# Funnel attention followed by a multiplicative FFN: one interleaved pipeline in place of three stages, with PV turned round and the transposes of its output done by DMA

## Chip, cores, metric

The kernel runs on one core of a Trainium2 chip. The metric is the device time of one execution in microseconds, measured on the chip; the profiles come from the hardware profiler, and in them time counts from the first instruction. Executions are called fast or slow: for a program on one core, slow means more than 1.5% above the fastest run of the same kernel.

Abbreviations: PE is TensorE (PEld its weight loads), DVE is VectorE, ACT is ScalarE, POOL is GpSimd, SP is SyncE; SPq is SP's issuing of DMAs. T is the product w3·w_out. A *pair* is two heads of one batch element; there are 32 pairs.

## The reference, cut to what matters

```python
# q, k, v: (8, 8, 1152, 64) float32, scaled by 0.1
q_pool = q.reshape(B, H, S // 2, 2, D).mean(axis=3)        # 576 queries
scores = q_pool @ k.T / sqrt(64)
attn   = softmax(scores)                                   # over 1,152 keys
x      = (attn @ v), heads side by side                    # (4608, 512)
a = x @ w1 ; b = x @ w2                                    # (4608, 1024)
out = ((a * b) @ w3) @ w_out                               # float32 (4608, 512)
```

Both kernels use that (a·b)·w3·w_out = (a·b)·T with T = w3·w_out, calculated once. Both calculate in fp16 with fp32 sums, and neither subtracts the maximum.

## The kernel before

There are three stages, one after the other. First T: w3 is transposed block by block on PE and multiplied by w_out. Then attention, by head pairs; this is the loop of one pair, shortened:

```python
# (cut: pools, tiles)
for h0 in range(0, H, 2):
    for b in range(B):
        # k, q, v of two heads: rows of 64 elements
        nc.gpsimd.dma_start(out=kpair[:, :, u, :], in_=k[b, h].rearrange("(c p) d -> p c d", p=128))
        # ... the same for q and v ...
        for jt in range(NJ):                       # nine transposes by DMA
            nc.sync.dma_start(out=kT2[:, jt, :], in_=kpair[:, jt, :, :], transpose=True)
        # pooling of q on PE (18 small matmuls), then one DVE copy to qpT2
        for g0 in range(0, FLAT, 512):             # 11 groups of 512 columns, two heads each
            # scores: k stationary (64 rows x 128), pooled q moving
            nc.scalar.activation(out=eT[...], in_=psc[...], func=AF.Exp, ...)
            for jt in range(done_av, jdone):       # PV at once: v stationary, exponentials moving
                nc.tensor.matmul(poT[u][:, i0:i0 + ln], vt_[u][:, jt, 0:D + 1], eT[...], ...)
        # result and sum of exponentials to DRAM
        nc.sync.dma_start(out=xT32d[h, :, b * Sq:(b + 1) * Sq], in_=otmp[0:64, :])
        nc.sync.dma_start(out=zAll[h, b * Sq:(b + 1) * Sq], in_=otmp[64:65, :])
    # every eight pairs: zAll back from DRAM, reciprocal, to DRAM, back as a broadcast;
    # xT32d back; product into xT (fp16, features on partitions)
```

Here PV gives 64 features on partitions and 576 queries along the free axis. The sum of exponentials of a query then lies in row 64, and must reach all 64 rows; this kernel sends it there through DRAM. The last stage is the FFN over nine units of 512 tokens, each 96 matmuls of 512 columns.

The softmax here doesn't subtract the row's maximum and nothing guards it: scores larger than these inputs give would overflow.

Of the kernel before, what the change touches and what calls it, by code (L numbers as in the profile page):

```python
# [7 lines left out]
DBG = set()  # L9

FP32 = mybir.dt.float32
FP16 = mybir.dt.float16
BF16 = mybir.dt.bfloat16
F32R = mybir.dt.float32r
AF = mybir.ActivationFunctionType
ALU = mybir.AluOpType


def _make_pool_matrix(nc, ptile):
    nc.gpsimd.memset(ptile, 0.5)  # L20
    nc.gpsimd.affine_select(
        out=ptile, in_=ptile, compare_op=ALU.is_ge, fill=0.0,
        base=0, channel_multiplier=1, pattern=[[-2, ptile.shape[1]]],
    )
    nc.gpsimd.affine_select(
        out=ptile, in_=ptile, compare_op=ALU.is_gt, fill=0.0,
        base=2, channel_multiplier=-1, pattern=[[2, ptile.shape[1]]],
    )


def _make_identity(nc, ident):
    nc.gpsimd.memset(ident, 0.0)
    nc.gpsimd.affine_select(
        out=ident, in_=ident, compare_op=ALU.not_equal, fill=1.0,
        base=0, channel_multiplier=1, pattern=[[-1, ident.shape[1]]],
    )


def _pieces(lo, hi, *bounds):
    cuts = set()  # L40
    for bnd in bounds:
        x = (lo // bnd + 1) * bnd
        while x < hi:
            cuts.add(x)
            x += bnd
    edges = [lo] + sorted(cuts) + [hi]
    return [(edges[i], edges[i + 1] - edges[i]) for i in range(len(edges) - 1)]


def _interleave(items, keyfn):  # L50
    ev = [x for x in items if keyfn(x) % 2 == 0]
    od = [x for x in items if keyfn(x) % 2 == 1]
    out = []
    for i in range(max(len(ev), len(od))):
        if i < len(ev):
            out.append(ev[i])
        if i < len(od):
            out.append(od[i])
    return out
# [3 lines left out]
def kernel(  # L63
# [12 lines left out]

    B, H, S, D = q.shape
    Sq = S // 2
    NJ = S // 128
    dm = H * D  # L80
    dff = moe_w1.shape[1]
    NT = B * Sq
    NC = dm // 128
    NF = dff // 128

    SCALE = float(D) ** -0.5
    SCL = 16.0
    AG = 1024
    NPSC = 2
    FLAT = NJ * Sq  # L90

    const = ctx.enter_context(tc.tile_pool(name="const", bufs=1))
    big = ctx.enter_context(tc.tile_pool(name="big", bufs=1))

    ident16 = const.tile([128, 128], FP16)
    _make_identity(nc, ident16)
    pool16 = const.tile([128, 64], FP16)
    _make_pool_matrix(nc, pool16)

    xT = big.tile([128, NC, NT], FP16)  # L100
    w1sb = big.tile([128, NC, dff], FP16)
    nc.gpsimd.dma_start(out=w1sb, in_=moe_w1.rearrange("(c p) f -> p c f", p=128))
    w2sb = big.tile([128, NC, dff], FP16)
    nc.gpsimd.dma_start(out=w2sb, in_=moe_w2.rearrange("(c p) f -> p c f", p=128))
    T16 = big.tile([128, NF, dm], FP16)

    zpool = ctx.enter_context(tc.tile_pool(name="zpool", bufs=1, space=bass.MemoryType.DRAM))
    zAll = zpool.tile([H, NT], FP32)
    xT32d = zpool.tile([H, 64, NT], FP32)


    with tc.tile_pool(name="t_sb", bufs=1) as tsb, \
         tc.tile_pool(name="t_ps", bufs=2, space=bass.MemoryType.PSUM) as tps:
        w3sb = tsb.tile([128, NF, dff], FP16)
        nc.gpsimd.dma_start(out=w3sb, in_=moe_w3.rearrange("(c p) f -> p c f", p=128))
        wosb = tsb.tile([128, NF, dm], FP16)
        nc.gpsimd.dma_start(out=wosb, in_=moe_w_out.rearrange("(c p) f -> p c f", p=128))
        w3T = tsb.tile([128, NF, dff], FP16)
        for a in range(NF):
            pt = tps.tile([128, 1024], FP32, tag="w3tp")  # L120
            for c in range(NF):
                nc.tensor.transpose(pt[:, c * 128: c * 128 + 128].bitcast(FP16)[:, 0:128],  # L122
                                    w3sb[:, c, a * 128: a * 128 + 128], ident16)
            nc.vector.tensor_copy(out=w3T[:, a, :], in_=pt.bitcast(FP16).rearrange("p (c j) -> p c j", j=256)[:, :, 0:128])
        for ft in range(NF):
            pT = tps.tile([128, dm], FP32, tag="pT")
            for a in range(NF):
                nc.tensor.matmul(pT, w3T[:, a, ft * 128: ft * 128 + 128], wosb[:, a, :],  # L128
                                 start=(a == 0), stop=(a == NF - 1))
            nc.scalar.copy(out=T16[:, ft, :], in_=pT)  # L130

    with tc.tile_pool(name="att_sb", bufs=2) as sb, \
         tc.tile_pool(name="att_sb3", bufs=3) as sb3, \
         tc.tile_pool(name="att_dram", bufs=4, space=bass.MemoryType.DRAM) as sdram, \
         tc.tile_pool(name="att_norm", bufs=1) as npool, \
         tc.tile_pool(name="att_ps", bufs=1, space=bass.MemoryType.PSUM) as ps:
        for h0 in range(0, H, 2):
            for b in range(B):
                hpair = [h0, h0 + 1]
                qt_, vt_ = [], []  # L140
                kpair = sb3.tile([128, NJ, 2, D], FP16, tag="kpair")
                for u, h in enumerate(hpair):
                    qtile = sb3.tile([128, NJ, D], FP16, tag=f"qtile{h % 2}")
                    vtile = sb3.tile([128, NJ, D + 1], FP16, tag=f"vtile{h % 2}")
                    nc.gpsimd.dma_start(out=kpair[:, :, u, :], in_=k[b, h].rearrange("(c p) d -> p c d", p=128))  # L145
                    nc.gpsimd.dma_start(out=qtile, in_=q[b, h].rearrange("(c p) d -> p c d", p=128))  # L146
                    nc.vector.memset(vtile[:, :, D:D + 1], 1.0)  # L147
                    nc.gpsimd.dma_start(out=vtile[:, :, 0:D], in_=v[b, h].rearrange("(c p) d -> p c d", p=128))  # L148
                    qt_.append(qtile); vt_.append(vtile)

                kT2 = sb3.tile([128, NJ, 128], FP16, tag="kT2")
                for jt in range(NJ):
                    nc.sync.dma_start(out=kT2[:, jt, :], in_=kpair[:, jt, :, :], transpose=True)  # L153

                pqpt = ps.tile([128, 1024], FP32, tag="psc", bufs=NPSC)
                pqp = pqpt[:, 0:Sq]
                for jt in range(NJ):
                    nc.tensor.matmul(pqp[0:64, jt * 64: jt * 64 + 64],  # L158
                                     qt_[0][:, jt, :], pool16, start=True, stop=True)
                    nc.tensor.matmul(pqp[64:128, jt * 64: jt * 64 + 64],  # L160
                                     qt_[1][:, jt, :], pool16, start=True, stop=True)
                qpT2 = sb3.tile([128, Sq], FP16, tag="qpT2")
                nc.vector.tensor_copy(out=qpT2, in_=pqp)

                eT = sb.tile([128, 2, FLAT], FP16, tag="eT")
                poT = [ps.tile([65, 1024], FP32, tag="poT", bufs=2, name=f"poT{_u}") for _u in range(2)]
                done_av = 0
                for g0 in range(0, FLAT, 512):
                    glen = min(512, FLAT - g0)
                    psc = ps.tile([128, 2, 512], FP32, tag="psc", bufs=NPSC)  # L170
                    for (st, ln) in _pieces(g0, g0 + glen, Sq):
                        jt = st // Sq
                        i0 = st - jt * Sq
                        for u in range(2):
                            nc.tensor.matmul(  # L175
                                psc[:, u, st - g0: st - g0 + ln],
                                kT2[u * 64: u * 64 + 64, jt, :],
                                qpT2[u * 64: u * 64 + 64, i0:i0 + ln],
                                start=True, stop=True)
                    nc.scalar.activation(out=eT[:, :, g0:g0 + glen], in_=psc[:, :, 0:glen],  # L180
                                         func=AF.Exp, bias=0.0, scale=SCALE)
                    jdone = (g0 + glen) // Sq
                    for jt in range(done_av, jdone):
                        for (i0, ln) in _pieces(0, Sq, 512):
                            for u in range(2):
                                nc.tensor.matmul(  # L186
                                    poT[u][:, i0:i0 + ln], vt_[u][:, jt, 0:D + 1],
                                    eT[:, u, jt * Sq + i0: jt * Sq + i0 + ln],
                                    start=(jt == 0), stop=(jt == NJ - 1))
                    done_av = jdone  # L190
# [26 lines left out]
    if "nomoe" in DBG:  # L217
        nc.vector.memset(out[0:128, :], 0.0) if False else None
        return
# [60 lines left out]
```

## Time and profile before

The median is 853.73 us (four runs, 849.86 to 854.45).

| Stage | us | PE busy | granted clock |
|---|---|---|---|
| weights and T | 0 to 50 | 41% | 1.0 |
| attention | 50 to 658 | about 67% | 0.73 |
| FFN | 658 to 853 | 96% | 0.98 |

The page of the kernel before, the rows of 40 equal slices (21.3 us each; a digit is a tenth):

```profile
PE   0777878866657885566788556568810899999998
...
PEclk9998876866666777766768877586865899999999
DMA  9999999999899999999989998963055011111111
```

PE is only full in the last quarter, the FFN. In attention its granted clock lies between a half and full, and the DMA row reads 8 or 9 until about 555 us. The windows of two stages of the kernel before (busy us, number of instructions, then clock, DMA share and GB/s):

```profile
50.00:650.00 600.00, 399.86 (x2868) 190.33 (x2868) 105.15 (x164) 321.18 (x352) 171.62 (x174) 0.73 1.05 104
660.00:853.00 193.00, 185.78 (x852) 83.53 (x851) 53.23 (x73) 63.61 (x108) 0.00 (x0) 0.98 0.13 50
```

The columns of busy time are PE, PEld, DVE, ACT, POOL. The DMA share is the sum of the times of packets over the time of the 16 engines, and can be above 1. The DMA queues of the kernel before (packets, MB, share of 16 engines), then its chain of waits by engine:

```profile
q0 software_dynamic: 227392, 33.57, 61.0%
q1 hardware_dynamic: 58944, 47.67, 25.2%
...
PE 47%; DMA 17%; ACT 13%; SPq 11%; DVE 6%; issue 4%; POOL 1%; DVEq 0%; ACTq 0%; POOLq 0%
```

The timeline of SP in the kernel before (start us, duration) shows nine transposes of a pair, then its stores:

```profile
113.41 11.33 SPq L153 DMA_TRANSPOSE kT_1174<-kpair  x9
124.84 0.53 SPq L196 DMA_DIRECT2D xT32d<-otmp  x1
125.42 0.43 SPq L197 DMA_DIRECT2D zAll<-otmp  x1
```

### The profile page before, as it was taken

To read this page: it belongs to the slowest core of one execution; us is meant where nothing else is said; L and a number is where in the kernel's file an instruction comes from. 1 tells how busy PE (TensorE), PEld (TensorE's weight loads), DVE (VectorE), ACT (ScalarE), POOL (GpSimd) and SP (SyncE) were. 2 spreads that over 40 slices of the span, in tenths; PEclk is the share of its full clock that TensorE was granted. 3 is DMA by queue.
4 is the path that set the end of the run, shared out by engine and by line. 5 is a ranking of instruction groups with operands and counts; after the bars stand their busy time and mean duration, and the time that the engine had idled before them with its cause. 6 is when DMAs were issued, how large, how long until landed. Compare 5 with 4: busy or idle time off the path is not lost.

```text
span 853.1 us, 10018 instructions
## 1 busy us (share of the span) xinstructions
PE 606.2 (71%) x3872; PEld 285.8 (33%) x3872; DVE 166.3 (19%) x252; ACT 391.5 (46%) x469; POOL 193.9 (23%) x205
## 2 busy tenths in 40 slices
PE   0777878866657885566788556568810899999998
PEld 0433433422323332232334222233300344444443
DVE  0211111103121111322211032220003322222222
ACT  0157656644445664444566444456600333333332
POOL 4512525342213243221324322020000000000000
PEclk9998876866666777766768877586865899999999
DMA  9999999999899999999989998963055011111111
GB/s 167 170 91 79 115 98 119 94 134 150 141 107 85 84 93 118 162 143 102 89 77 97 127 147 148 86 66 48 15 128 111 25 50 57 54 50 59 53 50 50
DMA packets 286384, 81.88 MB, mean 96 GB/s; under 512 B 273472, under 2 KB 274496, under 8 KB 285312
## 3 DMA queue, kind: packets, MB, share of 16 engines
q0 software_dynamic: 227392, 33.57, 61.0%
q1 hardware_dynamic: 58944, 47.67, 25.2%
q8 instruction: 30, 0.49, 0.2%
q14 instruction: 18, 0.15, 0.1%
HBM read 86.13 MB, written 19.17 MB: 123 GB/s over the span
## 4 chain that ended last, share of the span: by engine, by line
PE 47%; DMA 17%; ACT 13%; SPq 11%; DVE 6%; issue 4%; POOL 1%; DVEq 0%; ACTq 0%; POOLq 0%
ACT eT L180 13%; SPq L153 10%; PE psc L175 8%; PE pa L230 7%; PE po L244 7%; PE pb L234 7%; DMA zsb<-zAll 3%; DMA wosb<-in_moe_w_out_dram 3%; DVE xT L214 3%; PE pT L128 2%; DMA x_3888<-xT32d 2%; DMA x_1472<-xT32d 2%; DMA x_2680<-xT32d 2%; DMA x_5096<-xT32d 1%; DVE otmp L195 1%
## 5 line engine op out<-in xcount | busy, mean ns | idle before, releaser
L180 ACT ACTIVATE eT<-psc 128x1024 f16<-128x1024 f32 (+1 forms) x352 | 321.9, 954 | 249.0 <-PE psc L175 242.8
L186 PEld LDWEIGHTS <-vtile 128*65 128x65 f16 x1152 | 131.3, 127 | 221.7 <-issue 170.2
L145 POOL DMA_DIRECT2D kpair<-in_k_dram x64 | 63.8, 997 | 275.0 <-DMA zAll<-otmp 164.6
L230 PE MATMUL pa<-xT,w1sb 128*128 128x512 f16 x288 | 75.6, 384 | 42.1 <-DVE xT L214 40.6
L238 ACT COPY asb<-pa 128x512 f32<-128x512 f32 x72 | 42.1, 585 | 119.2 <-PE pa L230 119.2
L146 POOL DMA_DIRECT2D qtile<-in_q_dram x64 | 63.5, 1004 | 63.2 <-PE pqpt L160 57.5
L239 DVE TENSOR_TENSOR gT<-pb,asb 128x512 f16<-128x512 f32 x72 | 49.8, 691 | 130.0 <-PE pb L234 128.5
L234 PE MATMUL pb<-xT,w2sb 128*128 128x512 f16 x288 | 74.8, 381 | 0.0
L148 POOL DMA_DIRECT2D vtile<-in_v_dram x64 | 63.6, 999 | 42.2 <-DVE vtile L147 23.7
L244 PE MATMUL po<-T_75,gT 128*128 128x512 f16 x288 | 63.6, 379 | 0.0
L234 PEld LDWEIGHTS <-w2sb 128*128 128x128 f16 x288 | 28.3, 98 | 75.3 <-issue 41.8
L247 ACT ACTIVATE osb<-po 128x512 f32<-128x512 f32 x36 | 21.5, 597 | 49.0 <-PE po L244 47.0
L230 PEld LDWEIGHTS <-w1sb 128*128 128x128 f16 x288 | 28.4, 98 | 36.2 <-issue 3.0
L244 PEld LDWEIGHTS <-gT 128*128 128x128 f16 x288 | 28.1, 98 | 34.0
L122 PE MATMUL pt<-ident_61,w3sb 128*128 128x128 f16 x64 | 5.8, 259 | 25.5 <-DMA w3sb<-in_moe_w_dram 25.5
L130 ACT CAST T_75<-pT 128x512 f16<-128x512 f32 x8 | 4.7, 585 | 40.5 <-PE pT L128 40.5
L204 DVE RECIPROCAL rsb<-zsb 128x72 f32<-128x72 f32 x4 | 2.4, 603 | 75.1 <-DMA zsb<-zAll 75.1
L128 PE MATMUL pT<-wosb,w3T 128*128 128x512 f16 x64 | 14.6, 379 | 1.7 <-DMA wosb<-in_moe_w_out_dram 1.7
L158 PE MATMUL pqpt<-pool_66,qtile 128*64 128x64 f16 x288 | 15.0, 198 | 0.8 <-ACT T_75 L130 0.8
L160 PE MATMUL pqpt<-pool_66,qtile 128*64 128x64 f16 x288 | 15.1, 199 | 0.0
L122 PEld LDWEIGHTS <-w3sb 128*128 128x128 f16 x64 | 5.3, 119 | 26.3 <-DMA w3sb<-in_moe_w_dram 25.5
L175 PE MATMUL psc<-qpT_4082,kT_4053 64*128 64x512 f16 (+7 forms) x36 | 5.0, 360 | 12.3 <-DVE vtile L147 12.3
(250 smaller groups left out, 723.7 us busy)
## 6 DMA issues: line engine op xcount, KB each, us to landing
kpair<-in_k_dram POOLq DMA_DIRECT2D x64, 144.0 KB, 5.5
qtile<-in_q_dram POOLq DMA_DIRECT2D x64, 144.0 KB, 5.6
vtile<-in_v_dram POOLq DMA_DIRECT2D x64, 144.0 KB, 5.6
xT32d<-otmp SPq DMA_DIRECT2D x64, 144.0 KB
rb<-rAll SPq DMA_DIRECT2D x8, 1152.0 KB
out_dram<-osb SPq DMA_DIRECT2D x36, 256.0 KB
w3sb<-in_moe_w_dram POOLq DMA_DIRECT2D x1, 2048.0 KB, 21.7
x_1467<-xT32d SPq DMA_DIRECT2D x1, 1152.0 KB
```

What stands on the lines that cost most here:

```text
L145: nc.gpsimd.dma_start(out=kpair[:, :, u, :], in_=k[b, h].rearrange("(c p) d -> p c d", p=128))
L146: nc.gpsimd.dma_start(out=qtile, in_=q[b, h].rearrange("(c p) d -> p c d", p=128))
L148: nc.gpsimd.dma_start(out=vtile[:, :, 0:D], in_=v[b, h].rearrange("(c p) d -> p c d", p=128))
L153: nc.sync.dma_start(out=kT2[:, jt, :], in_=kpair[:, jt, :, :], transpose=True)
L175: nc.tensor.matmul(psc[:, u, st - g0: st - g0 + ln], kT2[u * 64: u * 64 + 64, jt, :], qpT2[u * 64: u * 64 + 64, i0:i0 + ln], start=True, s ...
L180: nc.scalar.activation(out=eT[:, :, g0:g0 + glen], in_=psc[:, :, 0:glen], func=AF.Exp, bias=0.0, scale=SCALE)
L186: nc.tensor.matmul(poT[u][:, i0:i0 + ln], vt_[u][:, jt, 0:D + 1], eT[:, u, jt * Sq + i0: jt * Sq + i0 + ln], start=(jt == 0), stop=(jt == ...
L230: nc.tensor.matmul(pa[:, 0:tl], w1sb[:, mc, ft * 128: ft * 128 + 128], xT[:, mc, t0: t0 + tl], start=(mc == 0), stop=(mc == NC - 1))
L234: nc.tensor.matmul(pb[:, 0:tl], w2sb[:, mc, ft * 128: ft * 128 + 128], xT[:, mc, t0: t0 + tl], start=(mc == 0), stop=(mc == NC - 1))
L238: nc.scalar.copy(out=asb[:, 0:tl], in_=pa[:, 0:tl])
L239: nc.vector.tensor_mul(out=gT[:, ft, 0:tl], in0=pb[:, 0:tl], in1=asb[:, 0:tl])
L244: nc.tensor.matmul(po[0:ttl, :], gT[:, ft, tt: tt + ttl], T16[:, ft, :], start=(ft == 0), stop=(ft == NF - 1))
```

## The change

The intent is to leave no stage in which PE waits:

- *Loads in wide rows.* A partition takes 9 (or 18) neighbouring rows of k, v (or q): 1,152 B or more in SBUF, where it was 128 B.
- *One transpose instruction* for the nine blocks of kT; pooling on DVE before a transpose of q.
- *PV turned round.* The exponentials are stationary (128 queries), v with its column of ones moves (65 columns). The result has queries on partitions, so 1/z is a per-partition number beside it. Normalisation is a reciprocal and a product on DVE; DMA transposes then write xT. Nothing goes through DRAM.
- *Lag.* A flat stream of 324 chunks of 512 columns over all pairs; PV runs one iteration (two chunks) behind the exponentials.
- *Weaving.* Batches come first, so tokens are complete early, and steps of T and of the FFN (four matmuls each) are put between attention steps, 1.2 per iteration. Seven of the nine units run inside the loop.

```diff
-                    nc.gpsimd.dma_start(out=kpair[:, :, u, :], in_=k[b, h].rearrange("(c p) d -> p c d", p=128))
+            out=kst[P].rearrange("p u j d -> p u (j d)"),
+            in_=k[b, h0:h0 + 2].rearrange("u (p j) d -> p u (j d)", j=NJ))
-                for jt in range(NJ):
-                    nc.sync.dma_start(out=kT2[:, jt, :], in_=kpair[:, jt, :, :], transpose=True)
+        nc.sync.dma_start_transpose(out=kT[P], in_=kc.rearrange("p j u d -> p (j u d)"))
...
-                                    poT[u][:, i0:i0 + ln], vt_[u][:, jt, 0:D + 1],
-                                    eT[:, u, jt * Sq + i0: jt * Sq + i0 + ln],
+        for u in range(2):
+            for i in range(5):
+                f = 128 * i if i < 4 else SQ - 128
+                nc.tensor.matmul(
+                    po[P][:, u, VW * i:VW * i + D + 1],
+                    er[:, u, r + f:r + f + 128],
+                    vts[P % 4][:, u, j, 0:D + 1], ...)
...
+        nc.vector.reciprocal(out=rz, in_=acc[:, :, :, D:D + 1])
+        nc.vector.tensor_tensor(out=xn..., in0=acc[:, :, :, 0:D], in1=rz.to_broadcast(...), op=ALU.mult)
+        nc.sync.dma_start_transpose(out=xT[:, hp, n0:n0 + 512]..., in_=xn[:, 0:4]...)
...
+    for it in range(NIT):                       # 162 iterations
+        if it == 3:
+            w3_transpose()                      # 2 DMA transposes of 32 blocks each, on SP
+        if it == 6:
+            filler.append(gen_T())
+        # (cut) a unit of the FFN joins the filler as soon as its tokens are complete
+        scores(2 * it)
+        expo(2 * it)
+        scores(2 * it + 1)
+        expo(2 * it + 1)
+        # (cut) loads and transposes two pairs ahead
+        credit = min(credit + 24 / 20.0, 2.4)
+        while (SQ * (nextJ + 1) - 1) // CH <= 2 * it - 1:
+            attend(nextJ)                       # PV of one block of keys
+            nextJ += 1
+        fill(3)                                 # steps of T and the FFN, by credit
```

## The prediction

> **What bounds the kernel now.** It has three stages in series. The timeline in 40 slices and the stage windows show: 0 to 50 us weights and the product w3·w_out; 50 to 658 us attention, 32 head pairs at about 19 us each; 658 to 853 us the FFN. Only the last is full: matmuls of 512 columns follow each other every 216 ns at a granted clock near 1.0. In attention PE is busy about 70% at a clock of 0.70 to 0.76, ACT 55%. The reasons there are data movement: DMA engines are 90% busy or more in nearly every slice, the software queue alone 61% of 16 engines (227,392 packets, nearly all under 512 B); each pair issues nine 128x128 DMA transposes of 1.23 us on SP, about 13.5 us with its stores; and four times a head pair's normalisation goes through DRAM (loads of zAll and xT32d, 7 to 13 us each in the chain of waits). The chain is PE 47%, DMA 17%, ACT 13%, SP queue 11%.
>
> **What the change does.** Loads become rows of 1,152 B in SBUF instead of 128 B, so the software queue should fall from 61% to a small share. The DRAM round trip of x, z and 1/z goes. PV is turned: 1,152 weight loads and 331,776 columns [...] become 2,880 pairs of weight load and 65-column matmul. In this trace 128x128 weight loads hide behind 128-column matmuls (56 ns pitch in the w3 transposes), and two 64-column pairs pass in about 30 ns (pooling). So I estimate 30 to 45 ns a pair, 86 to 130 us. A 128-wide weight load took 98 ns against about 110 for 65-wide ones[...]. Pooling leaves PE (288 pairs) for a DVE add. The FFN (864 matmuls, 187 us) is unchanged, but seven of nine units and T are woven into the attention loop.
>
> **Cost.** The loop has 162 iterations. ACT: two exponentials at 0.92 us pitch, 1.84 us. PE: scores 0.47, PV 0.55 to 0.8, 1.2 filler steps of 0.866: 2.05 to 2.3 us. So PE sets the pace just above ACT: 162 x 2.25 = 365 us, plus about 1 us a pair for the single po bank and DVE queueing: 32 us. Outside it: start until the first scores 17 us; a stall near pair 3, since the 64 blocks of the w3 transposes stand before its kT on SP, 25 us; the tail of two units and the rest of a third, 52 steps x 0.866 plus drains, 52 us. Sum 491 us. Nearly all of the gain lies on the critical path, because the old FFN stage stops being a stage.
>
> **Predicted: 490 us, 8 in 10 between 440 and 590.** Faster by over 2%: 0.96; within 2%: 0.02; slower: 0.02.
>
> **What would show it.** PE busy 80% or more in the loop, clock above 0.9; ACT about 80% there; DMA share about a third; one PV pair near 30 to 45 ns start to start; the tail near 50 us.
>
> **What would make it wrong.** SP. Per pair it now issues about 18 blocks' worth of transposes in four instructions. [...] If 1.23 us holds per 128x128 block, SP needs over 20 us a pair and the time is 700 us; if most of it is fixed per instruction, 8 to 10 us and it hides. No trace here tells which. Also PV pairs at 60 ns or more, or the clock falling to half in the loop (PE would then need 4 us an iteration), would add 50 to 150 us.

For the old PV the trace gives an estimate: at the 216 ns measured for 512 columns, its 331,776 columns take 140 us. That a transpose might cost by block stands as an assumption: before the change only the 1.23 us of one block was measured.

## More of the kernel before

The wait that costs PE most in attention, from the waits of PE in the kernel before (us in total, times, longest):

```profile
PE psc L175 <- DVE vtile L147: 108.8, 28, 12.3
```

At the start of nearly every pair PE waits for DVE, which copies the pooled queries behind the epilogue of the pair before. (The view names L147, the memset of a later v tile; in the timelines the copy, L163, ends 0.05 us before PE starts.) Most of these waits last 1.74 us.

Nine last 4.1 to 12.3 us, 75.7 us together, and they come three pairs in a row, at each of the first three ways through DRAM: in the timeline of DVE the copy stands, as in the program, behind an instruction of the way through DRAM that waits for its DMA (21.72 us in this one):

```profile
194.18 0.60 DVE L204 RECIPROCAL rsb<-zsb 128x72 f32<-128x72 f32 x1 [21.72 <-DMA zsb<-zAll]
...
195.97 0.74 DVE L163 CAST qpT_1666<-pqpt 128x576 f16<-128x576 f32 x1
```

PE starts the scores of that pair at 196.76 us, after 9.47 us idle. Elsewhere one pair follows the other every 14.6 to 17.4 us; those nine take 18.7 to 25.7 us.

## The result

The changed kernel takes 498.14 us (median of four, 497.42 to 498.83). The ratio to the kernel before is 0.5832 (95% interval 0.5811 to 0.5853). Ratios here are the mean time of one kernel's fast runs over that of the other's in the same rounds, so not quite the ratio of the medians quoted.

The page of the changed kernel, the same rows (slices of 12.4 us):

```profile
PE   0062009987999999999999999999999999999996
...
PEclk9996558998999999999999999999999999999998
DMA  8999999899899898999998989998999254012213
```

From the eleventh slice on PE is at 90% or more, but for the last. What is left lies at the start: in the first six slices, about 75 us, PE is busy for about 12 us. The windows of the loop and of the tail of the changed kernel (columns as above):

```profile
120.00:440.00 320.00, 311.49 (x3984) 160.44 (x3982) 148.51 (x252) 258.79 (x269) 42.87 (x63) 1.00 0.90 129
448.00:497.00 49.00, 43.76 (x202) 19.48 (x200) 13.03 (x19) 14.14 (x24) 0.00 (x0) 0.97 0.25 57
```

In the loop PE is busy 311.49 of 320 us, 97%, at full clock, and ACT 81%. The tail is 49 us. The queues and the chain of the changed kernel:

```profile
q0 software_dynamic: 25168, 33.56, 46.2%
q1 hardware_dynamic: 91840, 30.43, 39.8%
...
PE 69%; DMA 15%; ACT 7%; issue 5%; DVE 3%; POOL 1%; ACTq 0%; DVEq 0%; POOLq 0%
```

There are nine times fewer packets on the software queue, with the same bytes. Its share has only come down by a quarter, but of a shorter span: in time, 61.0% of 853 us was 520 us of packets and 46.2% of 497 us is 230 us. And what PE waited for most, from its waits in the changed kernel (us in total, times, longest):

```profile
PE psc L143 <- DMA qT<-qp: 32.3, 2, 25.7
PE pT L218 <- DMA w3T<-w3h: 28.5, 1, 28.5
```

The first line holds two waits, 25.7 us until the first scores and 6.6 us before the second pair. The second is one wait for the transposed w3.

Two timelines of the changed kernel show why. On PE, the first step of T, which the program puts behind iteration 6, waits for the transposed w3, and everything behind it in PE's order waits too:

```profile
45.55 0.73 PE L163 MATMUL po<-vt_77,er 128*128 128x65 f16 x10
74.76 1.89 PE L218 MATMUL pT<-wosb,w3T 128*128 128x512 f16 x4 [28.48 <-DMA w3T<-w3h]
```

On SP, the two long transposes of w3 stand behind qT of the third pair, and before kT and qT of the fourth (L105 and L123 below); PE waited for neither of these two.

```profile
35.45 9.50 SPq L123 DMA_TRANSPOSE qT<-qp  x1
44.99 31.93 SPq L204 DMA_TRANSPOSE w3T<-w3h  x2
77.04 1.20 SPq L180 DMA_TRANSPOSE xT<-xn  x1
78.28 1.23 SPq L183 DMA_TRANSPOSE xT<-xn  x1
79.62 1.29 SPq L105 DMA_TRANSPOSE kT<-kc  x1
80.96 1.27 SPq L123 DMA_TRANSPOSE qT<-qp  x1
```

The same lines settle the question that the prediction left open. A transpose of nine blocks (L105) holds SP for 1.29 us here; one of four blocks (L180) 1.20 us; one of half a block (L183) 1.23 us. Before, one block took 1.23 us. So, up to nine blocks, the time on SP does not go by block. It is no constant either. Over all 32 pairs the instruction of nine blocks took (the view of its line: shortest/median/longest in ns, then first and last start in us)

```profile
L105 SPq DMA_TRANSPOSE kT<-kc x32: 1295/2129/5904, 5.9 to 417.3; - x32
```

and at the start, where loads are queued as well, the one for qT took up to 10.85 us. From issue to landing qT took 2.7 us at the least, 6.8 us in the median and 23.9 us at the most. What held SP back was not isolated.

So the 497 us of the profiled span divide as follows: 26 us to the first scores, 35 us of two gaps, 387 us for the 162 iterations, 49 us of tail. Over iterations 24 to 140 the exponentials of successive iterations start 2.40 us apart on average.

Where do the 355 us come from? The FFN stage of 195 us is no longer a stage; the attention stage of 608 us has become a loop that contains most of the FFN. The profiles alone do not say what part of the change did how much. The experiments ask that.

### The profile page after: what moved, and what is told of

It reads as the page before. It is cut to its first block, busy times and chain, and to the rows that moved or that the text cites. A ratio compares the mean times of both kernels' runs of the same rounds, so it can differ in the third digit from the quotient of the medians.

```text
span 496.9 us, 11617 instructions
## 1 busy us (share of the span) xinstructions
PE 415.5 (84%) x4960; PEld 213.4 (43%) x4960; DVE 182.8 (37%) x313; ACT 327.2 (66%) x349; POOL 69.4 (14%) x105
## 3 DMA queue, kind: packets, MB, share of 16 engines
q0 software_dynamic: 25168, 33.56, 46.2%
## 4 chain that ended last, share of the span: by engine, by line
PE 69%; DMA 15%; ACT 7%; issue 5%; DVE 3%; POOL 1%; ACTq 0%; DVEq 0%; POOLq 0%
PE po L163 18%; PE psc L143 16%; PE pa L231 11%; PE pb L242 11%; PE pp L250 10%; ACT er L149 7%; DMA w3T<-w3h 6%; DMA w3h<-in_moe_w_dram 4%; DMA kst<-in_k_dram 2%; PE pT L218 2%; DVE xn L175 2%; DMA qst<-in_q_dram 2%; DVE rz L173 1%; DMA xT<-xn 0%; POOL kst L83 0%
## 5 line engine op out<-in xcount | busy, mean ns | idle before, releaser
L149 ACT ACTIVATE er<-psc 128x1024 f16<-128x1024 f32 x324 | 311.8, 1023 | 133.2 <-PE psc L143 132.8
L143 PE MATMUL psc<-qT,kT 64*128 64x512 f16 (+7 forms) x1152 | 114.5, 291 | 42.9 <-DMA qT<-qp 32.3
L163 PEld LDWEIGHTS <-er 128*128 128x128 f16 x2880 | 98.5, 98 | 48.4 <-issue 35.5
L143 PEld LDWEIGHTS <-kT 64*128 64x128 f16 x1152 | 44.3, 95 | 125.3 <-issue 91.9
L250 PE MATMUL pp<-T_73,gT 128*128 128x512 f16 x288 | 70.1, 379 | 0.0
L83 POOL DMA_DIRECT2D kst<-in_k_dram x32 | 23.2, 724 | 273.6 <-DVE kc L103 248.8
L238 DVE COPY asb<-pa 128x512 f32<-128x512 f32 x56 | 38.7, 691 | 57.8 <-PE pa L231 57.5
L218 PE MATMUL pT<-wosb,w3T 128*128 128x512 f16 x64 | 17.3, 400 | 28.5 <-DMA w3T<-w3h 28.5
L163 PE MATMUL po<-vt_77,er 128*128 128x65 f16 x720 | 31.2, 199 | 1.5 <-DVE xn L175 1.5
L163 PE MATMUL po<-vt_78,er 128*128 128x65 f16 x720 | 29.7, 194 | 0.9 <-DVE xn L175 0.9
L163 PE MATMUL po<-vt_80,er 128*128 128x65 f16 x720 | 29.4, 194 | 1.2 <-DVE xn L175 1.2
L163 PE MATMUL po<-vt_79,er 128*128 128x65 f16 x720 | 29.4, 194 | 1.2 <-DVE xn L175 1.2
L175 DVE TENSOR_TENSOR xn<-po,rz 128x640 f16<-128x640 f32 x32 | 26.4, 824 | 1.1
L90 POOL DMA_DIRECT2D vst<-in_v_dram x32 | 23.7, 740 | 13.7 <-DMA wosb<-in_moe_w_out_dram 7.3
```

The source lines that it names most:

```text
L83: nc.gpsimd.dma_start(out=kst[P].rearrange("p u j d -> p u (j d)"), in_=k[b, h0:h0 + 2].rearrange("u (p j) d -> p u (j d)", j=NJ))
L90: nc.gpsimd.dma_start(out=vst[P].rearrange("p u j d -> p u (j d)"), in_=v[b, h0:h0 + 2].rearrange("u (p j) d -> p u (j d)", j=NJ))
L143: nc.tensor.matmul(t[:, u, o:o + ln], kT[P][s, j, :], qv[s, f0:f0 + ln], start=True, stop=True)
L149: nc.scalar.activation(out=er[:, :, r:r + CH], in_=psc.pop(c), func=AF.Exp, bias=0.0, scale=SCALE)
L163: nc.tensor.matmul(po[P][:, u, VW * i:VW * i + D + 1], er[:, u, r + f:r + f + 128], vts[P % 4][:, u, j, 0:D + 1], start=(j == 0 and i == 0 ...
L175: nc.vector.tensor_tensor(out=xn.rearrange("p i u d -> p u i d"), in0=acc[:, :, :, 0:D], in1=rz.to_broadcast([128, 2, 5, D]), op=ALU.mult)
```

## The experiments

Seven kernels start from the changed kernel and undo one part or redo its start; five start from the kernel before and do one or more parts of the change alone. Each ran beside the kernel before on one chip (three chips in all), in 3 rounds or 5.

### What weaving is worth

```diff
-        while next_unit < n_units:
-            last_b ...
+        while False:          # all nine FFN units after the loop
```

> The changed kernel with all nine FFN units after the attention loop instead of seven of them inside. Theory A (the loop is bound by PE at 2.40 us an iteration, and falls to the pace of the exponentials, about 1.95 us, once the FFN is out): the loop from iteration 24 on loses 138 x 0.45 = 62 us, the tail grows from 49 to about 189 us: about 576 us. Rival B (weaving hid the FFN for nothing in time that PE had free): the loop keeps its time and the total is about 638 us. A third outcome, over 600 us with a granted clock near 0.5 to 0.75 in the loop, would say that the FFN also keeps PE's clock up.

Measured: 582.18 us, ratio 0.6823 (0.6788 to 0.6858). Theory A holds. The window of the loop in this run:

```profile
120.00:380.00 260.00, 192.75 (x3291) 123.77 (x3290) 56.02 (x114) 244.72 (x265) 42.62 (x63) 0.95 0.96 133
```

ACT is busy 244.72 of 260 us, 94%: the exponentials set the pace, and an iteration takes 1.98 us on average (1.81 at the least, two exponentials at 0.904 us). Weaving is thus worth 84 us, not the 140 us or more of the seven units that it moved, because PE time in the loop was not free beyond the difference between ACT's pace and PE's own work. The clock stayed at 0.95 in the loop although PE was busy only 74%; the third outcome of the expectation did not occur.

One more reading of this run: in its tail, where no attention matmul stands between them, FFN matmuls start 215.8 ns apart. Inside the loop of the changed kernel (iterations 24 to 140) they average 245 ns from each start to the next matmul's, so a step of four takes 0.98 us and not 0.866. The scores, too, take 0.33 us a chunk against the 0.235 that the prediction used. What takes the difference, no run here isolates.

### Whether turning PV pays on PE

```diff
-            for i in range(5):                       # exponentials stationary, v moving
+            jj = min(j, NJ - 2)
+            for i in range(2):                       # v stationary, exponentials moving
+                f, ln = (0, 512) if i == 0 else (512, 64)
                 nc.tensor.matmul(
-                    po[P][:, u, VW * i:VW * i + D + 1], er[:, u, r + f:r + f + 128],
-                    vts[P % 4][:, u, j, 0:D + 1], ...)
+                    po[P][:, u, 0:ln], vts[P % 4][:, u].rearrange("p j w -> p (j w)")[:, VW * jj:VW * jj + 128],
+                    er[:, u, r + f:r + f + ln], ...)
```

> Wrong result on purpose: PV turned back for its time alone, v stationary (128 columns), exponentials moving in 512 + 64 columns, four matmuls a block of keys instead of ten; the reciprocal becomes a multiplication so that nothing overflows. Theory A (the loop is bound by PE and the turned PV is cheaper, 10 x 31.6 ns = 316 ns a block against 4 matmuls and 1,152 columns = 490 ns): 288 x 174 ns = 50 us more, about 548 us. Rival B (the turn is neutral on PE and only changes the epilogue): within 2% of 498 us.

Measured: 537.01 us, ratio 0.6286 (0.6250 to 0.6322). (The result is wrong, as said.) The turn saves 39 us, less than the 50 us expected: with v stationary the score matmuls took 9 ns less each (83.6 against 92.8 ns from start to next start, iterations 24 to 140), about 10 us over all 1,152. In the changed kernel the matmuls of PV start 31.8 ns apart on average over these iterations (median 29), within the 30 to 45 ns of the prediction. The 128-wide weight loads of the exponentials take 97 ns each, but they too start 29 ns apart (both medians): they overlap.

### Whether the single transpose instruction matters

```diff
-        nc.sync.dma_start_transpose(out=kT[P], in_=kc.rearrange("p j u d -> p (j u d)"))
+        for j in range(NJ):
+            nc.sync.dma_start_transpose(out=kT[P][:, j, :], in_=kc[:, j].rearrange("p u d -> p (u d)"))
```

> The changed kernel with kT transposed in nine DMA instructions a pair, as before, instead of one. Theory A (SP pays about 1.25 us for each transpose instruction, whatever its number of blocks): SP needs 9 x 1.25 + 1.25 + 2.45 + about 1 us of stores = 16 us a pair, more than PE's 12.1, so the time is about 590 us, with PE waiting for kT. Rival B (the issue costs by block, so nine short ones cost as one long one): within 2% of 498 us.

Measured: 653.79 us, ratio 0.7658 (0.7621 to 0.7695). The direction and the mechanism are theory A's; the time is 64 us more than it said, because its sum left out the gaps of the start and because a pair takes 17.4 us instead of 16 (3.43 us an iteration). The timeline of SP in this run, and its chain of waits by engine:

```profile
318.89 12.68 SPq L106 DMA_TRANSPOSE kT<-kc  x9
331.62 1.31 SPq L124 DMA_TRANSPOSE qT<-qp  x1
...
SPq 38%; PE 31%; DMA 23%; issue 3%; DVE 2%; ACT 2%; POOL 0%; ACTq 0%; DVEq 0%; POOLq 0%
```

Nine instructions hold SP for 11.6 and 12.7 us in two pairs of this timeline, some six times the median of 2.13 us for the one, and SP leads the chain. Without this part of the change, the changed kernel would have lost almost half of its gain (155 of 355 us).

### Whether short packets limited anything: k and v again in rows of 64

```diff
-            out=kst[P].rearrange("p u j d -> p u (j d)"), in_=k[b, h0:h0 + 2].rearrange("u (p j) d -> p u (j d)", j=NJ))
+            out=kst[P][:, 0], in_=k[b, h0].rearrange("(j p) d -> p j d", j=NJ))      # and head h0 + 1; v alike
```

> The changed kernel with k and v loaded in rows of 64 elements again (147,456 packets of 128 B instead of 16,384 of 1,152 B), all else the same. Theory A (short packets had filled the DMA engines in the kernel before, at 32 ns a packet): they take 325 us of 16 engines, with q, transposes and weights over 500 us, so the loop becomes bound by DMA: 560 us or more, PE waiting for kT or qT in the loop. Rival B (in the kernel before the DMA share was queueing, and the serial waits cost the time): within 2% of 498 us.

Measured: 514.46 us over four runs from 505.65 to 529.03, two of them slow; the fast ones give a ratio of 0.5945 (0.5896 to 0.5994), 1.9% above the changed kernel's 0.5832. Theory A said 560 us or more, and falls. B is nearly right: the loss is small, though clear. The window of the loop in the profiled run (a slow one, so only its DMA share is used):

```profile
120.00:440.00 320.00, 296.87 (x3736) 152.21 (x3735) 142.68 (x238) 243.19 (x253) 101.63 (x110) 0.98 1.64 132
```

The DMA share reads 1.64, and the loop moves as many GB/s as before (132 against 129). A share that rises from 0.90 to 1.64 at nearly the same rate and time does not measure how full the engines are. The times of packets overlap. What costs the 1.9% was not separated: the edit also doubles the number of these loads, and POOL, which issues them, is busy 101.63 us where it was 42.87.

### The same question on the kernel before: wide rows alone

```diff
+                kst = sb3.tile([128, 2, NJ, D], FP16, tag="kst")       # and vst
+                nc.gpsimd.dma_start(out=kst..., in_=k[b, h0:h0 + 2].rearrange("u (p c) d -> p u (c d)", c=NJ))
+                nc.vector.tensor_copy(out=kpair.rearrange("p c u d -> p u c d"), in_=kst)   # v alike
```

> The kernel before, with k and v alone loaded in wide rows into a staging tile (1,152 B a row, as the changed kernel does) and copied by DVE: 147,456 short packets fewer. Theory A (the 61% share of the software queue was mostly packets overlapping and queueing; SP and the DRAM round trip set the pace of attention): within 5% of 853 us. Rival B (short packets were the limit of attention): 325 us of packet time fewer, so attention falls to SP's pace of about 14 us a pair: about 700 us.

Measured: 877.66 us, ratio 1.0285 (1.0232 to 1.0338): slower by 3%. Theory A holds. The software queue's share fell from 61.0% to 36.6%, for nothing. The loss of 26 us lies at the start. The DVE copies of k that wide rows need stand before the first copy of pooled queries, and wait there for DMAs, so PE waits 21.6 us before its first scores, where it waited 0.9 us. From the first pair to the last both kernels then take the same time (557.6 us here, 556.6 before): in the steady state wide rows neither gained nor lost.

### One transpose instruction alone, on the kernel before

```diff
-                for jt in range(NJ):
-                    nc.sync.dma_start(out=kT2[:, jt, :], in_=kpair[:, jt, :, :], transpose=True)
+                nc.sync.dma_start_transpose(out=kT2, in_=kpair.rearrange("p c u d -> p (c u d)"))
```

> The kernel before, with one transpose instruction a pair instead of nine. Theory A (SP pays about 1.25 us an instruction and 13.5 us of a pair's 19 us were SP's): SP falls to about 3.5 us a pair; PE and ACT work of a pair is about 13 us at that clock, so 4 to 5 us a pair, 130 to 160 us less: about 700 us. Rival B (loads of short rows or the round trip hold the pace): within 5% of 853 us.

Measured: 812.60 us, ratio 0.9516 (0.9471 to 0.9561). SP's time mattered, but for 41 us, under a third of what theory A said; rival B (within 5%) names the size better. The pair times show where: the nine long pairs shrank, and only one at each way through DRAM still takes over 20 us (22.2, 21.1 and 21.6); all others take 14.6 to 17.8 us, about as before. So SP's time cost something only beside the way through DRAM. The next two take the way through DRAM out.

### No way through DRAM, on the kernel before

```diff
-                    nc.vector.tensor_scalar_mul(out=otmp, in0=poT[u][:, 0:Sq], scalar1=SCL)
-                    # ... xT32d, zAll, zsb, rAll, rb, x32 and the product into xT ...
+                    nc.vector.tensor_scalar_mul(out=xT[hq * 64: hq * 64 + 64, hc, b * Sq:(b + 1) * Sq],
+                                                in0=poT[u][0:64, 0:Sq], scalar1=SCL / S)
```

> Wrong result on purpose: the kernel before without normalisation through DRAM; the unnormalised PV result goes straight into xT. Theory A (the chain of waits puts about 12% of the span on zsb, rAll, rb, the loads of xT32d and the product into xT, four times): about 750 us. Rival B (the round trips hid behind the next pairs, and the chain only shows one of several parallel waits): within 3% of 853 us.

Measured: 753.59 us, ratio 0.8823 (0.8781 to 0.8864), as theory A said. All pairs now take 15.7 to 17.0 us, and no wait of PE for DVE in attention lasts over 2.0 us. That accounts for about all of the gain: before, the nine long pairs took 62 us more than nine of 16 us, and PE waited 40.6 us for the last product into xT before the FFN. The result passes the comparison although the kernel divides by a constant: with inputs of this scale the softmax sums are nearly all equal to the number of keys. It is no valid kernel, and since it does no normalisation at all, the 98 us are the most that leaving DRAM out can bring.

### Both, and all three

> The kernel before with both one transpose instruction a pair and no normalisation through DRAM (valid only for inputs whose softmax sums are nearly equal). Theory A (the two gains of 41 and 98 us add, since they are waits in series): about 714 us. Rival B (with the round trip gone, SP's issue of transposes is already hidden, as PE and ACT now set the pace): within 2% of the 754 us of b4.

> The kernel before with wide rows for k and v as well: all three changes of its data movement in the old order of stages. Theory A (PE and ACT pass work back and forth in attention at a clock of 0.75 to 0.8, so that less data movement gains nothing more): within 3% of b5. Rival B (short rows become the limit once the other two are gone): 5% or more faster than b5. Either way the rest to 498 us is what weaving, the turned PV and the pooling on DVE bring.

Measured: 753.80 us for both (ratio 0.8821, 0.8782 to 0.8860), the same as without the way through DRAM alone; and 764.50 us with wide rows as well (0.8962, 0.8927 to 0.8998), again for a later first pair (10.6 us). So the gains do not add. Once the way through DRAM is gone, SP has time enough for nine transposes (rival B of the first, theory A of the second). All the data movement of the change, put into the old order of work, brings 853 down to about 754 us and no further. Something else then holds attention at about 16 us a pair. The window of attention in the kernel with both, and two of its waits:

```profile
60.00:550.00 490.00, 374.13 (x2746) 177.71 (x2747) 72.57 (x151) 305.90 (x335) 163.81 (x166) 0.77 0.90 69
...
ACT eT L179 <- PE psc L174: 182.0, 153, 3.6
...
PE psc L174 <- DVE vtile L147: 57.4, 29, 2.0
PE poT L185 <- ACT eT L179: 55.0, 136, 1.0
```

PE is busy 76% and ACT 62%, and each waits for the other: PV of a group waits for its exponentials, and the next exponentials wait for PE. At each pair PE stands still for 2 us until DVE has copied the pooled queries. And the mean clock is 0.77. The records of the clock show it at half for 45% of that window, in stretches of 6.8 or 10.2 us, about once a pair; no two matmul starts in attention lie over 2.2 us apart. What lowers the clock, no run here shows. At half clock a group takes 1.64 us on PE (295.33 to 296.97 us of the timeline, for one), and ACT waits; at full clock exponentials follow each other every 0.92 us.

Compare the loop without weaving (e1), with the same exponentials and no FFN either: 10.0 us a pair, clock 0.95, no stop over 1.2 us at a pair's end. Between the two lie the lag of PV behind the exponentials, the flat stream of chunks over pair borders, pooling on DVE, the turned PV, and T and the loads under way during attention. Together they bring the 172 us from 754 to 582 (753.80 less 582.18). How these 172 us divide among them was not separated. An estimate from the figures above: of 16 us a pair, 11 groups at 0.92 us make 10 us, the stop is 2 us, and the 7 us at half clock (45%) lose about 3 us (0.92 us a group in place of 1.64). Over 32 pairs the loss of clock would be about 100 of the 172 us and the stops 64; no run of its own shows it.

### The start, redone

The last question is what is left at the start of the changed kernel. The first try moves the weights' loads to later iterations and cuts the w3 transposes into eight instructions:

```diff
-    load_w()
-    load_w12()
...
-        if it == 3:
-            w3_transpose()                   # 2 x 32 blocks
-        if it == 6:
+        if it == 1:
+            load_w()
+        if it == 6:
+            load_w12()
+        if 12 <= it < 20:
+            w3_transpose(it - 12)            # 8 x 8 blocks
+        if it == 14:
             filler.append(gen_T())
```

> The changed kernel with its start redone: w3 and w_out loaded from iteration 1, w1 and w2 from iteration 6, and the w3 transposes in eight instructions of eight blocks, one an iteration from 12, T from iteration 14. Correct result expected. Theory A (the 26 us to the first scores and the two gaps of 7 and 29 us at the start come from weight loads that fill the DMA engines and from 32 us of w3 transposes that stand before kT on SP): the first scores at about 16 us, no gap over 5 us: 450 to 460 us. Rival B (the same DMA work is only shifted and blocks the loop later): over 480 us.

Measured: 492.86 us, ratio 0.5782 (0.5734 to 0.5830): about 1% better than the changed kernel, and the intervals overlap. The first scores came at 25 us as before. Theory A falls for this edit: loads issued by POOL run ahead of the iterations in whose place they stand in the program, since nothing ties POOL to them: the load of w3 was issued at 13.8 us, as before (14.1 us), and those of w1 and w2 about 5 us later than before.

The second try holds POOL back with one-element copies out of the exponentials' ring, and brings the weights in 20 pieces:

```diff
+        if it < 24:
+            # POOL waits here for the first exponential of this iteration
+            r0 = (2 * it * CH) % RING
+            nc.gpsimd.tensor_copy(out=tick[0:1, it:it + 1], in_=er[0:1, 0, r0:r0 + 1])
+            # then pairs 2 and 3 (it 0 and 3), or one piece of the weights
```

> The changed kernel with its loads paced: only pairs 0 and 1 are loaded at once; one-element copies by POOL out of the exponentials' ring hold back pairs 2 and 3 and the weights, which come in 20 pieces, one an iteration up to iteration 21; the w3 transposes in eight instructions from iteration 8, T from 16. Correct result expected. Theory A ([...]any load queued up slows kT, qT and w3T several times; s3 only moved the block of loads): first scores at 14 to 16 us, each early kT or qT landing in under 5 us, no gap over 4 us: 440 to 455 us. Rival B (the transposes are slow at the start for another reason, or the DMA work of the start is too much for the first 24 iterations): over 475 us, with waits for w3T or qT moved to later iterations.

Measured: 496.83 us over six runs (490.66 to 504.19, two of them slow); the ratio of the fast ones is 0.5797 (0.5767 to 0.5827), within error of the changed kernel. Half of theory A came true: the first scores came at 16.2 us, 9.5 us earlier; with the loads of only two pairs issued by then, the first two qT held SP for 2.59 and 1.28 us, where it was 4.05 and 10.85 us in the changed kernel. But rival B had the total: the gaps came back later, as soon as pieces of w3 and the loads of later pairs were under way. The timeline of SP in this run:

```profile
41.55 10.37 SPq L125 DMA_TRANSPOSE qT<-qp  x1
52.02 3.89 SPq L209 DMA_TRANSPOSE w3T<-w3h  x1
```

A transpose of q, which holds SP for 1.3 us in the median in the loop of the changed kernel (2.0 us in that of this one), takes 10.4 us here, beside loads. In the changed kernel, transposes move in 256 B packets of 18 ns (median), loads in packets of 107 ns (1,152 B) or 172 ns (2,048 B); how the engines divide themselves between the two was not shown. That loads slow a transpose is the author's reading of these times. So the start may simply have more DMA work than it has time, in whatever order. The third try tests that and takes DMA work away. It keeps the paced start and transposes w3 on PE, which is busy only 14.37 of the 30 us from 30 to 60 us in this run, as the kernel before did:

```diff
     def w3_transpose(c):
-        nc.sync.dma_start_transpose(out=w3T[:, c], in_=w3h[c // 4][:, c % 4])
+        pt = bank("w3t", False).bitcast(FP16)
+        for a in range(NF):
+            nc.tensor.transpose(pt[:, 128 * a:128 * a + 128],
+                                w3h[c // 4][:, c % 4, 128 * a:128 * a + 128], ident)
+        nc.vector.tensor_copy(out=w3T[:, c].rearrange("p a f -> p (a f)"), in_=pt)
```

> The paced start of s4 with the 64 blocks of w3 transposed on PE (eight blocks in each of iterations 10 to 17, through one bank and a DVE copy) instead of by DMA. Correct result expected. Theory A (what s4 still lost at the start, about 55 us of gaps up to iteration 24, is DMA work: by packet times about 98 us of 16 engines fall due before iteration 24, of which the w3 transposes are about 12 us, and they hold SP for 32 us before qT): the gaps after 50 us shrink by 15 to 30 us: 470 to 482 us. Rival B (the loads alone keep the DMA engines full, so the gaps stay and only change their name): over 488 us.

Measured: 481.86 us (six runs, 480.20 to 503.49, one slow), correct, ratio 0.5638 (0.5612 to 0.5664). Against the changed kernel's 0.5832 that is 3.3% less, so this version beats both. Iteration 24 begins at 89.5 us, after 101.4 in the try before and 117.9 in the changed kernel. The median lies at the upper edge of what theory A said. The windows from 30 to 60 us and of the loop of this kernel:

```profile
30.00:60.00 30.00, 17.37 (x268) 11.93 (x266) 8.38 (x15) 16.77 (x18) 11.73 (x25) 0.82 1.20 187
...
120.00:420.00 300.00, 292.43 (x3767) 151.24 (x3767) 138.58 (x235) 244.29 (x254) 39.14 (x58) 1.00 0.87 131
```

From 30 to 60 us PE works 17.37 us where it worked 8.89 us in the changed kernel; the loop is the same, 97% busy. PE still waits 38 us for qT in all, the first scores included, so the start is not yet solved.

## Why the prediction was right

*The time.* Predicted 490 us, range 440 to 590; measured 498.14. The four terms of the sum, predicted and measured: start 17 and 26 us; stall 25 and 35 us; loop 397 (365 and 32) and 387 us; tail 52 and 49 us. The start terms were too small by 19 us, the loop too large by 10. The stall was also another than the one forecast: not kT of pair 3 behind the w3 transposes, but PE itself waiting 28.5 us for the transposed w3, at the first step of T in the middle of the second pair, and 6.6 us for qT of that pair. That its size came near is partly luck.

*The loop.* That PE would set the pace just above ACT was right: 97% and 81% busy. The parts were less right than their sum. PV came out at the low end (0.57 us an iteration, 24 to 140); scores took 0.66 us instead of 0.47, and the filler 1.17 us instead of 1.04; no run isolates why. Together this is 2.40 us where 2.25 was forecast. On the other hand the "about 1 us a pair for the single po bank and DVE queueing" hardly exists: in the whole run PE waited 4.9 us for it. Two errors cancelled, which is luck.

*The marks to look for.* PE over 80%, clock over 0.9, ACT about 80%, a PV pair at 30 to 45 ns, a tail near 50 us: all seen. "DMA share about a third" was wrong: it is 0.90 in the loop.

*What was wrong in the reasons.* "The reasons there are data movement: DMA engines are 90% busy or more in nearly every slice." The runs show otherwise. Wide rows in place of short ones gained nothing in the old order of work and at most 1.9% in the new; the share of packet time can read 1.64 without the time moving much. Of the other two reasons named, nine transposes were worth 41 us alone, and nothing beside the other; the way through DRAM was worth 98 us. Together these are 99 us, about 28% of the 355 us gained. The remaining 256 us came with the rest of the rebuilding: 172 us lie between the old order of work without those losses and the unwoven loop (seamless, lagging, with its turned PV, at clock 0.95), and no run divides them; 84 us are shown for weaving in the FFN. The prediction's total was right since it summed the new kernel's own work, and did not subtract the old one's supposed losses.

*The warning about SP.* It was the right place to look. Up to nine blocks the cost goes by instruction and not by block (medians: 1.22 us for half a block, 1.23 for one in the kernel before, 1.19 for four, 2.13 for nine, whose shortest was 1.30; also 1.30 for nine in the kernel before with one transpose), so SP hides in the loop: the four transposes of a pair hold it for about 6 us of 12 (sum of their medians); with nine instructions more time is lost, 155 us. Only at the start, beside loads, did the transposes hold SP for long (31.93 us for the two of w3, of 32 blocks each: 4.3 and 27.5 us), and that is where the stall was undersized.

## What to carry to other kernels

Predict a rebuilt kernel by adding up its own work stage by stage, and test the losses of the old one separately: parts of a change do not add, and here two of the three improvements of data movement were worth nothing once the third was in (753.59 us with it alone, 753.80 with the single transpose added, 764.50 with wide rows as well). Look for the stretches where the old loop is slow before naming a cost by iteration: the way through DRAM cost only nine pairs of 32 (62 us), and the end of attention (40.6 us). A DMA share near or over 100% did not show here that the engines were the limit: the loop read 0.90 in one kernel and 1.64 in another, at 129 and 132 GB/s, and their fast runs differ by 1.9%; only a change of the load told. Software-pipeline across the borders of the outer loop: with one transpose and no way through DRAM the old order still stopped PE for 2 us at each pair, the loop without weaving for no more than 1.2 us. At the start count the DMA work due before the first full iteration, and move what you can of it to an engine that is idle: with the w3 transposes on PE, 496.83 us became 481.86.
